# Keeping TensorE's instructions in emitted order in a fused block attention and feed-forward kernel

## The chip, the cores and the metric

The kernel runs on one core of one Trainium2 chip. The metric is device time in microseconds (us) of one execution; the time before is 1272.79 us, the median of 3 runs (1271.26 to 1273.68).

## The reference

Attention over 8 batches and 8 heads, 576 tokens, head size 64, with a mask by blocks of 64; its output, 4608 rows of 512, goes through a feed-forward layer with 2048 hidden units and a piecewise activation.

```python
def _attn_ref(q, k, v):                       # (8, 8, 576, 64), block = 64
    ...
    scores = scale * np.matmul(q, k.transpose(0, 1, 3, 2))
    ...
    mask = block_i >= block_j
    scores = np.where(mask, scores, -1000000000.0)
    scores = scores - np.max(scores, axis=-1, keepdims=True)
    attn = np.exp(scores)
    attn = attn / (np.sum(attn, axis=-1, keepdims=True) + 1e-09)
    return np.matmul(attn, v).astype(np.float32)

def _moe_ref(x, w_in, w_out):                 # (4608, 512), (512, 2048), (2048, 512)
    h = x @ w_in
    ...
    g = np.where(pos, h, np.where(neg, 0.0, (h + beta) ** 2 / (4.0 * beta)))
    return (g @ w_out).astype(np.float32)
```

The weights come as float64 and are converted on the core.

## The kernel before

The kernel works on 32 pairs of heads: 8 batches times 4 pairs. `attention_steps` is a generator that emits a pair in eight steps, each ended by a `yield`; work of the next pair (`nxt`) and the end of the last one (`old`) is mixed in by hand. The steps call these methods of `Pair`:

- `turned(is_q, j)`, line 341: four TensorE transposes (L346) of Q or K of head j into a PSUM tile `ps_qk`; ScalarE casts it to `qb` or `kb` (L351), and a DMA copies half of that to `qa` or `ka` (L357). `turned_last`, L365, does the last 64 rows of both heads.
- `scores(j, g)`, line 403: matmuls (L391, L394) into `ps_s`, VectorE's negated maximum (L414), ScalarE's exponential with its sum (L418), VectorE's reciprocal (L400, L401) and scaling (L424). From batch 1 on the result goes through a DMA to a rounded copy (`prr`, L246; in batch 1 `prs`, `pre` or the idle `vsr`, L239). `scores_last` is the same for the last 64 rows.
- `turn(j, g)` and `turn_last`: TensorE transposes of the probabilities (L461, in batch 0 L463) into `ps_t`, then a split into high and low parts on ScalarE (L454) and VectorE (L456).
- `attn_v` and `attn_v_first`: the weighted sums (L500) into `ps_av`, which become columns of `xh` and `xl`, the input of the feed-forward layer.

The feed-forward layer is a second generator. It works on chunks of 512 rows (9) and blocks of 128 hidden units (16 for each chunk). `ffn_in` is twelve matmuls (L646) into `ph`, then ScalarE (L655), VectorE (L656, L659), ScalarE (L660) and GpSimd (L661) make `gh` and `gl`, and a DMA fetches `wo` (L663). `ffn_out` is twelve matmuls (L670, L675) into four `po` banks. From the fifth step of the fifth pair on (`START`), one `ffn_in` or one `ffn_out` is emitted behind each attention step; what is left follows at the end. A third generator, `prepare_weights`, converts the weights (lines 152 to 184) beside batches 0 and 1 on ScalarE, VectorE and GpSimd.

PSUM has eight banks: three of the tag `work`, which `ps_qk`, `ps_s`, `ps_t` and `ps_av` take in turn, one for `ph`, four for `po` (lent to the attention before feed-forward begins). A tile gets its bank when the last reader of the bank's earlier tile is done.

The code only emits instructions. Their order on each engine's queue is set afterwards by an ordering tool: it takes, per engine, what it reckons to be ready first, by its own estimate of times, and otherwise what was emitted first. Each queue then runs strictly in that order. So an instruction can stand ahead of one that was emitted before it.

The sixth step of a pair is the one that the prediction speaks of most:

```python
            cur.scores(1, 1)
            cur.turn_last()
            if nxt:
                nxt.turned(False, 0)
            yield
```

Behind it the feed-forward generator emits twelve `ph` matmuls or twelve `po` matmuls.

Of the kernel before, what the change touches and what calls it, by code (L numbers as in the profile page):

```python
# [23 lines left out]
def block_attn_then_ffn(  # L24
# [59 lines left out]


    ident_f = ffn.tile([P, 512], F32, tag="t", name="ident_f")[:, :P]
    make_identity(nc, ident_f)
    ident_r = const.tile([P, P], F32R, tag="ident", name="ident_r")
    nc.vector.tensor_copy(ident_r, ident_f)
    ident = ident_r.bitcast(F32)  # L90

    xh = const.tile([P, NCC, RING], F32R, tag="xh", name="xh")
    xl = const.tile([P, NCC, RING], F32R, tag="xl", name="xl")
    wih = const.tile([P, NCC, DF], F32R, tag="wih", name="wih")
    wil = const.tile([P, NCC, DF], F32R, tag="wil", name="wil")
    wo_split = dram.tile([NFC, P, 2, DM], F32, tag="wo_split", name="wo_split")
# [3 lines left out]
    qa = const.tile([P, 2, QW], F32R, tag="qa", name="qa")  # L100
    qb = const.tile([P, 2, QW], F32R, tag="qb", name="qb")
    ka = const.tile([P, 2, S], F32R, tag="ka", name="ka")
    kb = const.tile([P, 2, S], F32R, tag="kb", name="kb")

    def last_blocks(t_):

        view = t_[:, :, SM : SM + BLK]
        if t_.shape[2] == S:
            return view
        part, (_, two), cols = view.ap  # L110
        return bass.AP(tensor=view.tensor, offset=view.offset, ap=[part, [QW + BLK, two], cols])


    mrow = att1.tile([NTL, 2, S], F32R, tag="pb0", name="mrow")


    pcs = [const.tile([P, 2, BLK], F32R, tag=f"pcs{i}", name=f"pcs{i}") for i in range(2)]
    vsr = [const.tile([P, NTL + 1, 2, D], F32R, tag=f"vsr{j}", name=f"vsr{j}") for j in range(2)]

    mtmp = ffn.tile([P, 512], F32, tag="t", name="mtmp")  # L120
    msel = ffn.tile([P, 512], F32, tag="t", name="msel")
    nc.vector.memset(mtmp, 0.0)
    nc.vector.memset(msel[:NTL], 0.0)
    nc.gpsimd.affine_select(
        out=msel[:NTL, : NTL * BLK].rearrange("p (t c) -> p t c", c=BLK),
        in_=msel[:NTL, : NTL * BLK].rearrange("p (t c) -> p t c", c=BLK),
        compare_op=ALU.not_equal, fill=1.0, base=0,
        pattern=[[-1, NTL], [0, BLK]], channel_multiplier=1,
    )
    sel = msel[:NTL, : NTL * BLK].rearrange("p (t c) -> p t c", c=BLK)  # L130
    for side in range(2):
        nc.vector.tensor_copy(mrow[:, side, :512], mtmp[:NTL, :512])
        nc.vector.tensor_copy(mrow[:, side, 512:S], mtmp[:NTL, : S - 512])
    rows = mrow[:, :, :SM].rearrange("p s (t c) -> p s t c", c=P)
    nc.vector.tensor_copy(rows[:, 0, :, :BLK], sel)
    nc.vector.tensor_scalar_mul(rows[:, 1, :, BLK:], sel, MASKED)
    for t_ in (qa, qb):
        nc.vector.tensor_copy(
            t_[:, :, SM:], mtmp[:, : 2 * (QW - SM)].rearrange("p (h c) -> p h c", h=2)
        )  # L140
    for t_ in pcs:
        nc.vector.tensor_copy(t_[BLK:], mtmp[BLK:, : 2 * BLK].rearrange("p (h c) -> p h c", h=2))
    for t_ in vsr:
        nc.vector.tensor_copy(
            t_[BLK:, NTL, :, :], mtmp[BLK:, : 2 * D].rearrange("p (h c) -> p h c", h=2)
        )
    for j in range(2):
        nc.sync.dma_start(qa[D:KA, j, :S].bitcast(F32), mrow[:, 0, :].bitcast(F32))
        nc.sync.dma_start(ka[D:KA, j, :].bitcast(F32), mrow[:, 1, :].bitcast(F32))


    def convert(n, source, hi, lo, done):

        if n < BORROW and n % 2:
            bits = ffn.tile([P, CW, 2], I32, tag="t", name="bits")
            work = ffn.tile([P, 2, CW], F32, tag="gl", name="work")
        else:
            bits = conv.tile([P, CW, 2], I32, tag="bits", name="bits")
            work = conv2.tile([P, 2, CW], F32, tag="work", name="work")
        nc.sync.dma_start(bits, source.bitcast(I32).rearrange("p (n t) -> p n t", t=2))  # L160
        top, mag = work[:, 0, :], work[:, 1, :].bitcast(U32)
        low = bits[:, :, 0]


        nc.scalar.mul(top, bits[:, :, 1].bitcast(F32), 2.0**-112)
        nc.scalar.mul(low, low.bitcast(U32), 2.0**-29)
        nc.vector.tensor_scalar(
            out=top, in0=top, scalar1=F32_TOP, scalar2=-F32_TOP, op0=ALU.min, op1=ALU.max
        )
        nc.vector.tensor_scalar(  # L170
            out=mag, in0=top.bitcast(U32), scalar1=3, scalar2=None, op0=ALU.logical_shift_left
        )
        nc.vector.scalar_tensor_tensor(
            out=mag, in0=top.bitcast(U32), scalar=0x80000000, in1=mag,
            op0=ALU.bitwise_and, op1=ALU.bitwise_or,
        )
        yield
        w32 = mag.bitcast(I32)
        nc.gpsimd.tensor_tensor(out=w32, in0=w32, in1=low, op=ALU.add)  # L179
        w32 = w32.bitcast(F32)  # L180
        nc.scalar.copy(hi(), w32)
        yield
        nc.gpsimd.tensor_tensor(out=lo(), in0=w32, in1=hi().bitcast(F32), op=ALU.subtract)
        if done:
            done()

    def weight_pieces():

        for f0 in range(0, DF, CW):
            fs = slice(f0, f0 + CW)  # L190
            for cc in range(NCC):
                yield (
                    w_in[cc * P : (cc + 1) * P, fs],
                    lambda cc=cc, fs=fs: wih[:, cc, fs], lambda cc=cc, fs=fs: wil[:, cc, fs], None,
                )
            for fc in range(f0 // P, (f0 + CW) // P):
                ws = {}

                def part(w, d0, ws=ws):
                    if not ws:  # L200
                        ws[0] = ffn.tile([P, 2, DM], F32R, tag="wo", name="ws")
                    return ws[0][:, w, d0 : d0 + CW]

                for d0 in range(0, DM, CW):
                    yield (
                        w_out[fc * P : (fc + 1) * P, d0 : d0 + CW],
                        lambda p_=part, d0=d0: p_(0, d0), lambda p_=part, d0=d0: p_(1, d0),
                        None if d0 + CW < DM else
                        lambda fc=fc, ws=ws: nc.sync.dma_start(wo_split[fc], ws[0].bitcast(F32)),
                    )  # L210

    def prepare_weights():

        live = []
        for n, piece in enumerate(weight_pieces()):
            live = [c for c in live + [convert(n, *piece)] if next(c, True) is None]
            yield
        for _ in range(LAG):
            live = [c for c in live if next(c, True) is None]
            yield  # L220
# [3 lines left out]
    spare = {"n": 0, "of": []}  # L224

    def as_float32r(src, plain):

        if plain:
            if not spare["of"]:
                spare["of"] = [t_[:, :NTL, :, :].rearrange("p t h d -> p (t h d)") for t_ in vsr]  # L230
                spare["of"].append(att1.tile([P, S], F32R, tag="x32", name="prs")[:, :TCH])
                spare["end"] = att1.tile([P, G0 + P], F32R, tag="pa11", name="pre")[:, :BLK]
            moved = [spare["of"][spare["n"] % 3]]
            spare["n"] += 1
            if src.shape[1] > TCH:
                moved.append(spare["end"])
            for i, dst in enumerate(moved):
                n = min(TCH, src.shape[1] - i * TCH)
                nc.sync.dma_start(dst[:, :n].bitcast(F32), src[:, i * TCH : i * TCH + n])  # L239
            return moved  # L240
        moved = []
        for c0 in range(0, src.shape[1], TCH):
            n = min(TCH, src.shape[1] - c0)
            pool, tag = ((conv, "bits"), (conv2, "work"))[c0 > 0]
            dst = pool.tile([P, TCH], F32R, tag=tag, name="prr")
            nc.sync.dma_start(dst[:, :n].bitcast(F32), src[:, c0 : c0 + n])  # L246
            moved.append(dst)
        return moved


    class Pair:


        GROUPS = (((0, 0), (1, P)), ((2, 0),), ((3, 0),))

        def __init__(self, b, hp):
            self.b, self.hp = b, hp

            self.plain = b < PLAIN
            self.first = b == 0 and hp == 0  # L260

# [467 lines left out]
    for _ in ffn_steps:  # L729
        pass  # L730
# [30 lines left out]
```

## Time and profile before

| | |
|---|---|
| median of 3 runs | 1272.79 us (1271.26 to 1273.68) |
| profiled execution | 1272.09 us, its span 1270.3 us |
| TensorE matmuls | 1210.7 us busy, 95% of the span |
| TensorE weight loads | 1018.4 us, 80% |
| VectorE / ScalarE / GpSimd | 856.4 / 701.3 / 456.3 us |
| granted TensorE clock, mean | 0.985 |

The page has one profiled execution. PE is TensorE's matmuls, PEld its weight loads, DVE VectorE, ACT ScalarE, POOL GpSimd, SP the queue that issues the DMAs. A row of the timeline has start, duration, engine, line, operation, output and inputs, the shape, how many such instructions are merged, and in brackets how long the engine stood idle before and who released it. Matmuls are pipelined: one that is shown as 0.39 us is followed by the next after 0.23, so "busy" overlaps and says that TensorE had work, not how fast it went.

### The profile page before, as it was taken

Reading aid. Unit: us, or ns where it says so; the run is one execution under the profiler, and the core shown is the slowest. Engines: PE = TensorE matmul, PEld = TensorE weight load, DVE = VectorE, ACT = ScalarE, POOL = GpSimd, SP = SyncE. Lnnn points to the kernel's source line nnn. Section 1 sums busy time; section 2 is a strip of 40 time slices with the busy share of each in tenths; the row PEclk is TensorE's granted clock in tenths of the full one; section 3 lists DMA queues with packets and bytes.
Section 4 is the critical chain, followed back from the end, with each engine's and each line's share of the span. In section 5 each row is a group of like instructions: output and inputs, shape, how many; then the busy total and the mean of one; then the engine's idle time right before and its main releaser. Section 6 shows DMA issues by size and latency. Waiting matters only on the chain.

```text
span 1270.3 us, 20591 instructions
## 1 busy us (share of the span) xinstructions
PE 1210.7 (95%) x6496; PEld 1018.4 (80%) x6496; DVE 856.4 (67%) x2164; ACT 701.3 (55%) x1827; POOL 456.3 (36%) x454
## 2 busy tenths in 40 slices
PE   5879887899999999999999999999999999999998
PEld 4667666688888888888888888888888888888886
DVE  8998877857776777777777777777777676222222
ACT  5877656546565655566556656555565564222222
POOL 3555655523332333333333333333333332222222
PEclk9888989899999999999999999999999999999999
DMA  5656666655444545564455545454445443322432
GB/s 157 182 165 213 196 228 210 212 184 173 148 152 147 191 144 161 158 193 149 148 162 168 178 141 161 153 181 143 152 154 184 151 132 117 127 92 97 133 100 100
DMA packets 146093, 201.30 MB, mean 158 GB/s; under 512 B 63152, under 2 KB 93872, under 8 KB 145984
## 3 DMA queue, kind: packets, MB, share of 16 engines
q1 hardware_dynamic: 145984, 199.98, 50.4%
q8 instruction: 52, 0.85, 0.3%
q14 instruction: 57, 0.47, 0.1%
HBM read 120.59 MB, written 17.83 MB: 109 GB/s over the span
## 4 chain that ended last, share of the span: by engine, by line
PE 68%; DVE 8%; ACT 4%; issue 3%; DMA 3%; POOL 2%; SPq 0%; ACTq 0%; POOLq 0%; DVEq 0%
PE ph L646 26%; PE po L670 16%; PE po L675 8%; PE ps_av L500 7%; PE ps_t L461 3%; PE ps_s L394 3%; PE ps_s L391 3%; ACT pr L418 2%; PE ps_qk L346 2%; DMA prr<-pr 2%; DVE t L656 2%; DVE nm L414 1%; DVE t L659 1%; DVE pr L424 1%; POOL work L179 1%
## 5 line engine op out<-in xcount | busy, mean ns | idle before, releaser
L661 POOL TENSOR_TENSOR gl<-t,gh 128x512 fp32r<-128x512 f32 x144 | 186.9, 1298 | 604.7 <-ACT gh L660 301.8
L670 PE MATMUL po<-wo,gh 128*128 128x512 f32 x1152 | 296.9, 399 | 0.1
L656 DVE SCALAR_TENSOR_TENSOR t<-t 128x512 f32<-128x512 f32 x144 | 112.9, 784 | 200.2 <-ACT t L655 198.5
L646 PE MATMUL ph<-xh,wih 128*128 128x512 f32 x576 | 237.6, 413 | 2.7 <-DVE t L659 1.8
L670 PEld LDWEIGHTS po<-wo,gh 128*128 128x128 f32 x1152 | 207.7, 188 | 39.3 <-ACT gh L660 0.6
L646 PE MATMUL ph<-xl,wih 128*128 128x512 f32 x576 | 227.4, 395 | 0.9 <-DVE xl L536 0.9
L646 PE MATMUL ph<-xh,wil 128*128 128x512 f32 x576 | 227.4, 395 | 0.0
L655 ACT ACTIVATE t<-ph 128x512 f32<-128x512 f32 x144 | 86.1, 598 | 184.7 <-PE ph L646 184.7
L418 ACT ACTIVATE pr<-ps_s,nm 128x128 f32<-128x128 f32 (+3 forms) x256 | 134.4, 529 | 50.6 <-DVE nm L414 50.3
L414 DVE TENSOR_REDUCE nm<-ps_s 128x1 f32<-128x128 f32 (+3 forms) x256 | 123.6, 485 | 48.7 <-PE ps_s L394 47.4
L675 PE MATMUL po<-wo,gl 128*128 128x512 f32 x576 | 155.3, 391 | 0.0
L660 ACT CAST gh<-t 128x512 fp32r<-128x512 f32 x144 | 89.6, 622 | 102.1 <-DVE t L659 101.7
L391 PE MATMUL ps_s<-ka,qa 68*128 68x288 f32 (+4 forms) x384 | 122.5, 334 | 9.1 <-ACT kb L351 4.2
L646 PEld LDWEIGHTS ph<-xh,wil 128*128 128x128 f32 x576 | 109.1, 189 | 24.1
L675 PEld LDWEIGHTS po<-wo,gl 128*128 128x128 f32 x576 | 108.1, 188 | 23.3
L646 PEld LDWEIGHTS ph<-xh,wih 128*128 128x128 f32 x576 | 109.1, 189 | 21.7 <-DVE t L659 2.4
L646 PEld LDWEIGHTS ph<-xl,wih 128*128 128x128 f32 x576 | 109.6, 190 | 20.2 <-DVE xl L536 1.5
L394 PE MATMUL ps_s<-kb,qb 128*128 128x288 f32 (+4 forms) x384 | 121.4, 323 | 0.0
L454 ACT CAST pb<-ps_t 128x512 fp32r<-128x512 f32 (+1 forms) x120 | 65.5, 546 | 85.6 <-PE ps_t L461 83.8
L424 DVE TENSOR_SCALAR pr<-pr,sm 128x128 f32<-128x128 f32 (+3 forms) x256 | 104.8, 430 | 4.0
L336 POOL TENSOR_TENSOR vsr<-vn,vsr 64x64 fp32r<-64x64 f32 (+1 forms) x96 | 72.8, 768 | 88.6 <-ACT vsr L335 88.6
L456 DVE TENSOR_TENSOR pb<-ps_t,pb 128x512 fp32r<-128x512 f32 (+1 forms) x120 | 75.6, 630 | 40.4 <-ACT pb L454 39.9
(101 smaller groups left out, 1961.4 us busy)
## 6 DMA issues: line engine op xcount, KB each, us to landing
wo<-wo_split SPq DMA_DIRECT2D x144, 512.0 KB, 3.4
prr<-pr SPq DMA_DIRECT2D x96, 192.0 KB, 2.7
prr<-pr SPq DMA_DIRECT2D x72, 256.0 KB, 2.6
out_dram<-ob SPq DMA_DIRECT2D x36, 256.0 KB, 3.9
qn<-in_q_dram SPq DMA_DIRECT2D x32, 256.0 KB, 2.9
kn<-in_k_dram SPq DMA_DIRECT2D x32, 256.0 KB, 2.9
bits<-in_moe_w_in_dram SPq DMA_DIRECT2D x32, 256.0 KB, 3.6
bits<-in_moe_w_out_dram SPq DMA_DIRECT2D x32, 256.0 KB, 3.2
```

The lines of the kernel that those rows point to most:

```text
L391: nc.tensor.matmul(ps, qa[:KA, j, c0 : c0 + P], ka[:KA, j, k0 : k0 + n], start=first, stop=False)
L394: nc.tensor.matmul(ps, qb[:, j, c0 : c0 + P], kb[:, j, k0 : k0 + n], start=False, stop=last)
L414: nc.vector.tensor_reduce(out=nm[:, i : i + 1], in_=ps[:, cs], axis=AX.X, op=ALU.max, negate=True)
L418: nc.scalar.activation(pr[:, cs], ps[:, cs], AF.Exp, bias=nm[:, i : i + 1], scale=1.0, accum_out=sm[:, i : i + 1],)
L424: nc.vector.tensor_scalar_mul(pr[:, cs], pr[:, cs], sm[:, i : i + 1])
L500: nc.tensor.matmul(ps[:, lo_col:], vt, x, start=first and i == 0 and m == 0, stop=last and i == len(parts) - 1 and m == len(mov) - 1,)
L646: nc.tensor.matmul(ph, w[:, cc, fs], x[:, cc, xs], start=(cc == 0 and i == 0), stop=(cc == NCC - 1 and i == 2),)
L656: nc.vector.scalar_tensor_tensor(out=t_, in0=t_, scalar=1.0, in1=t_, op0=ALU.min, op1=ALU.mult)
L660: nc.scalar.copy(gh, t_)
L661: nc.gpsimd.tensor_tensor(out=gl, in0=t_, in1=gh.bitcast(F32), op=ALU.subtract)
L670: nc.tensor.matmul(po[tt], gh[:, ts_], wo[:, w, :], start=(fc == 0 and w == 0), stop=False)
L675: nc.tensor.matmul(po[tt], gl[:, ts_], wo[:, 0, :], start=False, stop=fc == NFC - 1)
```

## The change

The body of the kernel, from the first tile to the last loop, is put into a context that tells the ordering tool to keep the emitted order on TensorE, for the whole program. Nothing is added or removed, and the code inside is only indented; each line number grows by one. The other queues are still ordered by the tool, which now reckons with TensorE's fixed order.

```diff
+    with tc.manual_schedule(engines={mybir.EngineType.PE}):
 ...
-    ident_f = ffn.tile([P, 512], F32, tag="t", name="ident_f")[:, :P]
+        ident_f = ffn.tile([P, 512], F32, tag="t", name="ident_f")[:, :P]
 ...
```

What moves on TensorE's queue: 6386 matmuls stand on it in both. In batches 2 to 7 one group of four moves in each pair, and the other four queues have the same rows in the same order there. In batches 0 and 1 more moves, and the other queues change too.

TensorE, the sixth step of a pair in batches 2 to 7, before. `ps_s` of 384 columns are the scores of `scores(1, 1)`, `ps_t` the transposes of `turn_last`, `ps_qk<-ks` those of `turned(False, 0)`, `ph` the matmuls of `ffn_in`, of which twelve belong to this step:

```order
L391 MATMUL ps_s<-ka,qa 128x384
L394 MATMUL ps_s<-kb,qb 128x384
L461 MATMUL ps_t<-ident_r,prr 128x128 x4
L461 MATMUL ps_t<-ident_r,prr 64x128
L646 MATMUL ph<-xh,wih 128x512
L646 MATMUL ph<-xl,wih 128x512
L646 MATMUL ph<-xh,wil 128x512
L646 MATMUL ph<-xh,wih 128x512
L646 MATMUL ph<-xl,wih 128x512
L646 MATMUL ph<-xh,wil 128x512
L346 MATMUL ps_qk<-ident_r,ks 128x128 x4
```

The same place now:

```order
L392 MATMUL ps_s<-ka,qa 128x384
L395 MATMUL ps_s<-kb,qb 128x384
L462 MATMUL ps_t<-ident_r,prr 128x128 x4
L462 MATMUL ps_t<-ident_r,prr 64x128
L347 MATMUL ps_qk<-ident_r,ks 128x128 x4
L647 MATMUL ph<-xh,wih 128x512
L647 MATMUL ph<-xl,wih 128x512
L647 MATMUL ph<-xh,wil 128x512
```

The K transposes moved ahead of six `ph` matmuls; in 17 of the 23 pairs it is six, in the other 6 it is seven. Behind them all twelve `ph` follow.

TensorE in batch 0, second pair, before. Here `turn(0, 2)` has its `ps_t` at L463, and three `ph` of the first `ffn_in`, which is emitted in the fifth pair, stand among the attention of the second:

```order
L346 MATMUL ps_qk<-ident_r,qs 128x128 x4
L646 MATMUL ph<-xh,wih 128x512
L646 MATMUL ph<-xl,wih 128x512
L463 MATMUL ps_t<-ident_r,pr 128x128 x4
L391 MATMUL ps_s<-ka,qa 128x384
L394 MATMUL ps_s<-kb,qb 128x384
L646 MATMUL ph<-xh,wil 128x512
```

The same place now:

```order
L464 MATMUL ps_t<-ident_r,pr 128x128 x4
L347 MATMUL ps_qk<-ident_r,qs 128x128 x4
L392 MATMUL ps_s<-ka,qa 128x384
L395 MATMUL ps_s<-kb,qb 128x384
L464 MATMUL ps_t<-ident_r,pr 128x128 x4
```

The transposes of Q moved behind those of `turn(0, 2)`. The twelve `ph` of the first `ffn_in`, three in each of the second to the fifth pair, moved together to the fifth step of the fifth pair, where they are emitted.

TensorE in batch 1, fourth pair, second step, before (`po` are the twelve matmuls of `ffn_out`, `ps_av` the weighted sums):

```order
L461 MATMUL ps_t<-ident_r,prs 128x128 x4
L391 MATMUL ps_s<-ka,qa 128x384
L394 MATMUL ps_s<-kb,qb 128x384
L365 MATMUL ps_qk<-ident_r,qs 128x128
L365 MATMUL ps_qk<-ident_r,ks 128x128
L646 MATMUL ph<-xh,wih 128x512
```

The same place now:

```order
L462 MATMUL ps_t<-ident_r,prs 128x128 x4
L671 MATMUL po<-wo,gh 128x512 x8
L676 MATMUL po<-wo,gl 128x512 x4
L392 MATMUL ps_s<-ka,qa 128x384
L395 MATMUL ps_s<-kb,qb 128x384
L366 MATMUL ps_qk<-ident_r,qs 128x128
L366 MATMUL ps_qk<-ident_r,ks 128x128
```

The twelve `po` moved ahead of the scores; before, they stood behind seven `ph` and six weighted sums.

More of the change, by code (lines that the diff above doesn't have):

```diff
@@ L141, in block_attn_then_ffn @@
[L141 to L194, printed above, removed]
-                )
[L196 to L209, printed above, removed]
-                    )
@@ L212, in prepare_weights @@
[L212 to L248, printed above, removed]
@@ L496, in weighted @@
-        def weighted(self, ps, j, parts, first=True, last=True):
-            for i, (kt, lo_col, mov) in enumerate(parts):
-                vt = self.vs[j][: (BLK if self.plain and kt == NTL else P), kt, :, :]
-                for m, x in enumerate(mov):
-                    nc.tensor.matmul(
-                        ps[:, lo_col:], vt, x,
-                        start=first and i == 0 and m == 0,
-                        stop=last and i == len(parts) - 1 and m == len(mov) - 1,
-                    )
@@ new lines, in block_attn_then_ffn @@
+        START = 8 * NPAIR + 4
+        GROUP = CW // P
+        PART = NCC + GROUP * DM // CW
+        EARLY = 24
+        LAG = 2
+        weights = prepare_weights()
+        ffn_steps = feed_forward()
+        converted = 0
+        for i, _ in enumerate(attention_steps()):
+            if i < START:
+                want = (i + 1) * EARLY // START
+            else:
+                want = max(
+                    EARLY + (i - START + 1) * (NFC // GROUP * PART - EARLY) // (2 * NFC - 4 * GROUP),
+                    ((i - START) // (2 * GROUP) + 1) * PART,
+                )
+            want += LAG
+            for _ in range(want - converted):
+                next(weights, None)
+            converted = max(converted, want)
+            if i >= START:
+                banks["free"] = False
+                next(ffn_steps, None)
```

981 lines of the change are left out of this document (529 added, 452 removed).

## The prediction

> **What bounds the kernel now.** I read the page first: busy shares, the slices over time, and the chain that ended last.
>
> ```profile
> PE 1210.7 (95%) x6496; PEld 1018.4 (80%) x6496; DVE 856.4 (67%) x2164; ACT 701.3 (55%) x1827; POOL 456.3 (36%) x454
> PE   5879887899999999999999999999999999999998
> PEclk9888989899999999999999999999999999999999
> PE 68%; DVE 8%; ACT 4%; issue 3%; DMA 3%; POOL 2%; SPq 0%; ACTq 0%; POOLq 0%; DVEq 0%
> ```
>
> TensorE is 95% busy and holds 68% of the chain, but not evenly: the first nine slices (about 290 us) have gaps and a lower clock, the rest has neither. So I cut the span into five stretches: the attention before feed-forward begins, the rest of the fifth pair, where it begins, then up to the first moved K transposes of batch 2, from there to the end of attention, and feed-forward alone.
>
> ```profile
> 0.00:112.00 112.00, 84.36 (x440) 68.39 (x440) 99.45 (x307) 81.63 (x245) 55.92 (x76) 0.91 0.60 174
> 112.00:126.00 14.00, 12.83 (x64) 10.30 (x65) 11.40 (x33) 10.96 (x32) 5.92 (x7) 0.88 0.66 222
> 126.00:290.00 164.00, 145.87 (x716) 115.47 (x716) 123.60 (x303) 96.92 (x271) 84.96 (x99) 0.96 0.64 203
> 290.00:1064.00 774.00, 766.40 (x4376) 658.09 (x4375) 561.90 (x1428) 460.11 (x1190) 261.97 (x237) 1.00 0.51 159
> 1064.00:1271.00 207.00, 201.19 (x904) 166.16 (x903) 60.03 (x97) 51.65 (x92) 47.54 (x37) 1.00 0.33 108
> ```
>
> The columns after the length are PE, PEld, DVE, ACT and POOL busy, the granted clock, DMA. In the first, VectorE is busy 99.45 of 112 us and TensorE 84.36: there TensorE waits for others. From 290 to 1064 us TensorE is busy 766.40 of 774 us at the full clock, VectorE 562: any microsecond that TensorE loses there is added to the end. Its waits in that stretch, from the view of waits (longest in total first, weight loads):
>
> ```profile
> PEld ps_qk L346 <- ACT pr L418: 10.7, 20, 0.7
> PEld ps_t L461 <- PE ps_s L394: 2.7, 4, 1.0
> PEld ps_t L461 <- ACT pr L418: 2.0, 2, 1.5
> ```
>
> One wait stands out, 20 times about half a microsecond: the transposes of K (L346) for ScalarE's exponential (L418). That is exactly the place which the change moves. Here is one instance, from the timeline:
>
> ```profile
> 626.14 0.34 PE L394 MATMUL ps_s<-kb,qb 128*128 128x384 f32 x1
> 626.32 0.52 PE L461 MATMUL ps_t<-ident_r,prr 128*128 128x128 f32 x5
> 626.67 0.46 PE L646 MATMUL ph<-xh,wih 128*128 128x512 f32 x1
> 626.98 0.40 PE L646 MATMUL ph<-xl,wih 128*128 128x512 f32 x1
> 627.11 0.55 DVE L414 TENSOR_REDUCE nm<-ps_s 128x1 f32<-128x384 f32 x1
> 627.70 0.58 ACT L418 ACTIVATE pr<-ps_s,nm 128x384 f32<-128x384 f32 x1 [0.29 <-DVE nm L414]
> 627.90 0.40 PE L646 MATMUL ph<-xh,wil 128*128 128x512 f32 x1
> 628.18 0.19 ACT L418 ACTIVATION_READ_ACCUMULATOR pr<-ps_s,nm 128x1 f32 x1
> 628.42 0.40 PEld L346 LDWEIGHTS ps_qk<-ident_r,ks 128*128 128x128 f32 x4 [0.56 <-ACT pr L418]
> 628.80 0.47 PE L646 MATMUL ph<-xh,wih 128*128 128x512 f32 x1
> 630.03 0.40 PE L646 MATMUL ph<-xh,wil 128*128 128x512 f32 x1
> ```
>
> The three `work` banks of PSUM rotate. The scores at 626.14 took one, the two `ps_t` tiles at 626.32 the others, so the K transposes need the bank of the scores, and it is free only when the exponential has read it, at 628.37. In between TensorE ran six `ph` matmuls (626.67 to 627.90, one per 0.23 us), then waited the remaining half microsecond.
>
> **The change in batches 2 to 7.** The emitted order has no `ph` between the `ps_t` transposes and the K transposes. The release at 628.37 does not depend on the `ph`: reduction and exponential hang on the scores of 626.14 alone, and on rows of VectorE and ScalarE that stand in the same order as before. So TensorE reaches the K transposes at about 626.65 and stands until 628.42, 1.8 us in place of 0.56; then all twelve `ph` follow in place of six. The end of the twelfth moves by six spacings, 6 x 0.23 = 1.37 us. Queued behind the wait are the twelve `ph`, the next scores and the weighted sums; ScalarE's L655 and the rest of the feed-forward chain wait for the `ph` and shift as a whole. The transposes issue no DMA; the copy of K that follows their cast starts as long after the scores as before.
>
> Some pairs hoisted seven `ph`:
>
> ```profile
> 559.34 0.53 PE L461 MATMUL ps_t<-ident_r,prr 128*128 128x128 f32 x5
> 559.70 0.45 PE L646 MATMUL ph<-xh,wih 128*128 128x512 f32 x1
> 560.96 0.20 ACT L418 ACTIVATION_READ_ACCUMULATOR pr<-ps_s,nm 128x1 f32 x1
> 561.15 0.39 PE L646 MATMUL ph<-xh,wih 128*128 128x512 f32 x1
> 561.20 0.50 PEld L346 LDWEIGHTS ps_qk<-ident_r,ks 128*128 128x128 f32 x4
> 561.38 0.46 PE L346 MATMUL ps_qk<-ident_r,ks 128*128 128x128 f32 x4
> ```
>
> Here the bank was free at 561.16, just before TensorE came, so the K transposes can start 0.18 us earlier than they did, and seven spacings (1.61) come behind them: +1.43 us; where the release came later than this it is the full 1.6. How many pairs there are: the transposes of L346 for K in this stretch are
>
> ```profile
> L346 PE MATMUL ps_qk<-ident_r,ks x184: 221/248/285, 290.9 to 1044.1; 128*128 128x128 f32 x184
> ```
>
> 184 = 23 pairs x 2 heads x 4, and one of the two heads is moved in each (the other already stands where it was emitted). By the order seventeen of the 23 had six `ph` ahead, six had seven: 17 x 1.37 + 6 x 1.5 = 32.3 us; in two of the seventeen the bank was free a tenth of a microsecond early, which takes off 0.2. I take **+32**. It is given back only if another TensorE wait shrinks: the other waits of the stretch are small (2.7, 2.0 and less above) and start from TensorE's own scores, so I count nothing. The far ends: if the release came as early as the bare reduction and exponential allow after the scores (0.34 + 0.55 + 0.58 + 0.19 = 1.66 us after 626.14, so 0.57 us sooner than now), the 23 waits would be 0.57 shorter, 13 us in all: +19. Above, +32 plus the clock (below).
>
> On gaps the row of 626 to 628 is to be weighed against the Trainium skill, "TensorE: Matmul & The Clock Gate", section "Why this matters for your kernels": keep gaps between bursts of matmuls under about 3 us, or the clock halves. By that rule gaps of 1.8 us are free of any further price and +32 stands.
>
> **The change in the first 290 us.** Two terms. First, the first feed-forward unit:
>
> ```profile
> 0.00:112.00 112.00, 4.34 (x12) 1.95 (x12) 0.91 0.60 174
> ```
>
> Its twelve `ph` (this view is of L646 alone) ran in gaps of the first 112 us; now they stand in the pair at 112 to 126 us, where TensorE is busy 12.83 of 14 us. They cost from 0 (into its waits) over 2.7 us (12 x 0.23) to 5.2 (at half clock, 0.43 each, below). I take 2. What leaves the first 112 us gains nothing, since TensorE waits there; nor do the scores that now stand ahead of the K transposes. Second, from 126 to 290 us, 29 matmuls of `ph` and `po` that were hoisted over late transposes and weighted sums go back behind them: at most 29 x 0.23 = 6.7 us. Against that, twelve `po` now stand ahead of these scores, which waited long:
>
> ```profile
> 222.51 0.29 PEld L391 LDWEIGHTS ps_s<-ka,qa 68*128 68x128 f32 x1 [4.03 <-ACT kb L351]
> ```
>
> They may fill up to 12 x 0.23 = 2.8 us of it, or wait for their own `wo`. From -2.8 to +6.7 I take +2, for TensorE idles 18 of 164 us there and later waits take up part of a delay. VectorE's, ScalarE's, GpSimd's and SP's rows change their order here too (conversions against softmax); no row prices that, I give it +-6. Together **+4**, between -8 and +17.
>
> **Sum.** The profiled execution took 1272.1 us (span 1270.3): 1272.1 + 32 + 4 = 1308.1. The median shown is 0.7 above it: **1309 us**.
>
> **Rivals.**
> *Half clock.* The granted clock dropped after stretches in which TensorE streamed little:
>
> ```profile
> 177.73:181.14 3.41, 1.36 (x6) 0.84 (x6) 3.38 (x6) 1.87 (x6) 3.41 (x5) 1.00 0.91 290
> 181.14:184.55 3.41, 3.14 (x6) 2.16 (x7) 3.41 (x9) 1.35 (x6) 2.70 (x3) 0.50 0.17 55
> 205.04:208.45 3.41, 2.41 (x13) 1.76 (x14) 3.34 (x10) 1.75 (x6) 2.62 (x4) 1.00 0.86 270
> 181.41 0.90 PE L500 MATMUL ps_av<-pb,vs 128*128 128x320 f32 x1 [1.80 <-ACT pr L418]
> ```
>
> Six matmuls in 3.41 us (four `ph`, two transposes), with a wait of 1.80, were followed by 3.41 us at 0.50; thirteen in 3.41 us were not. In the changed kernel TensorE streams nothing but nine transposes from 626.31 to 628.80; a stretch of 3.41 us around this has room for (3.41 - 2.49) / 0.23 = 4 large matmuls: at the edge. If it trips, it does so for the 27% of the pairs whose 3.41 us contain the whole gap (0.92 / 3.41), six pairs, each losing half of 3.41 us: +10, **1319 us**. For it: the row of 181.14, which the rule quoted above would not give (its wait is 1.80 us). Against: the nine transposes may count as work. The same page, section "PE-mode transpose", says that transposes do not count as busy in the same way, which speaks for this rival.
>
> *Faster.* The first 290 us contain 47 us in which TensorE is idle (290 - 84.36 - 12.83 - 145.87); the emitted order puts ready scores ahead of transposes that wait, as at 222.51. Were all 47 us given back, the time would be 1272.8 + 32 - 47 = **1258 us**; it decides from 35 us on, three quarters of it. Against it: VectorE is busy 99.45 of the first 112 us, which no order of TensorE shortens.
>
> *A dear opening.* If the waits at the late transposes add up and the other queues turn worse, the opening costs 13 in place of 4: **1318 us**.
>
> *Shorter release.* +19 in place of +32, the far end above: **1296 us**.
>
> *No change.* TensorE's new waits would have to be hidden; with 766.40 of 774 us busy nothing hides them. **1273 us.**
>
> **How the numbers follow.** Forecast, 1302 to 1315: 0.58. Half clock 0.20, a dear opening 0.09, shorter release 0.06, faster 0.04, no change 0.03. Within 0.2% is what a measurement of this kernel cannot tell from no change. So faster 0.04, same 0.03, slower 0.93. The range leaves out the two last and the lower half of the release case, and half of a dear opening that also trips the clock: 1298 to 1324.
>
> **What would show it.** In the changed profile: the wait of the K transposes for L418 at about 1.7 us, 23 times, some 40 us in all in place of 10.7; twelve `ph` in one run behind them; TensorE's busy time from 290 us to the last pair unchanged, that stretch 32 us longer; the granted clock 1.00 in it (else the first rival). The tail of feed-forward alone stays at 207 us. I am wrong if the exponential releases the bank at another distance from the scores, or if the first 290 us change by more than 10 us.

## The result, and the profile after

The changed kernel takes 1331.66 us (1328.48 to 1334.08) against 1272.59 us for the kernel before, run on the same chip: a ratio of 1.0463, with an interval of 1.0433 to 1.0493. It is 59 us slower; 36 were forecast. Lines of the changed code are one higher than before (L346 is L347, L418 is L419). Its profiled execution took 1329.46 us, the span 1327.7. Both profiles have 6496 matmul records on TensorE, not the 6386 given with the change. Of all runs named below one, of e10_turned_fill, took 2360.20 us, nearly twice the three others of that kernel, and no figure here contains it. The page of the changed kernel, busy time and the two rows of TensorE over the slices:

```profile
PE 1223.2 (92%) x6496; PEld 1033.5 (78%) x6496; DVE 850.7 (64%) x2164; ACT 702.0 (53%) x1827; POOL 456.0 (34%) x454
PE   5866988899999999999999999999999999999998
PEclk9888988999999999999999999999999999999999
```

To see where the 57.4 us between the two spans lie, I cut both at the same two points: the first and the last of the moved K transposes. The view by stretches of the kernel before, with the columns as in the prediction:

```profile
0.00:290.90 290.90, 243.97 (x1222) 194.86 (x1223) 235.34 (x643) 190.41 (x550) 146.80 (x181) 0.94 0.63 193
290.90:1043.90 753.00, 746.99 (x4271) 641.56 (x4270) 545.47 (x1390) 447.60 (x1156) 256.39 (x231) 1.00 0.52 160
1043.90:1270.30 226.40, 219.69 (x1007) 182.01 (x1005) 75.56 (x133) 63.26 (x123) 53.12 (x42) 1.00 0.33 108
```

And of the changed kernel:

```profile
0.00:304.00 304.00, 242.54 (x1215) 196.46 (x1215) 231.73 (x642) 191.64 (x550) 146.75 (x181) 0.92 0.60 184
304.00:1101.00 797.00, 760.76 (x4275) 654.72 (x4276) 543.49 (x1390) 446.87 (x1156) 256.19 (x231) 0.98 0.49 152
1101.00:1327.70 226.70, 219.90 (x1008) 182.34 (x1007) 75.48 (x133) 63.46 (x123) 53.05 (x42) 1.00 0.33 108
```

The opening is 13.1 us longer, the steady part 44.0, the end 0.3. The row of the steady part splits further by itself. TensorE's idle time there went from 753.00 - 746.99 = 6.0 to 797.00 - 760.76 = 36.2 us: 30.2 us of waiting. Its busy time went up by 13.8 us for the same matmuls, and the granted clock from 1.00 to 0.98: the work itself ran slower. One pair of the changed kernel shows both, in the timeline of TensorE:

```profile
691.45 0.34 PE L395 MATMUL ps_s<-kb,qb 128*128 128x384 f32 x1
691.63 0.53 PE L462 MATMUL ps_t<-ident_r,prr 128*128 128x128 f32 x5
693.81 0.54 PE L347 MATMUL ps_qk<-ident_r,ks 128*128 128x128 f32 x4 [1.65 <-ACT pr L419]
694.72 0.40 PE L647 MATMUL ph<-xh,wil 128*128 128x512 f32 x1
694.95 0.40 PE L647 MATMUL ph<-xh,wih 128*128 128x512 f32 x1
696.42 0.63 PE L647 MATMUL ph<-xl,wih 128*128 128x512 f32 x1
696.85 0.63 PE L647 MATMUL ph<-xh,wil 128*128 128x512 f32 x1
```

The K transposes wait 1.65 us for the exponential. All 23 of them, in the view of waits from 250 to 1130 us:

```profile
PEld ps_qk L347 <- ACT pr L419: 39.2, 23, 2.1
```

That is the wait that was forecast. But from 695.2 us on the same `ph` matmul comes every 0.43 us in place of 0.23. The stretches around it, of 3.41 us each:

```profile
691.81:695.22 3.41, 1.76 (x14) 1.43 (x13) 2.70 (x9) 1.99 (x5) 0.00 (x0) 1.00 0.66 211
695.22:698.64 3.42, 3.42 (x10) 2.68 (x9) 0.00 (x0) 0.00 (x0) 0.00 (x0) 0.50 0.35 101
698.64:702.05 3.41, 3.41 (x23) 3.07 (x22) 2.72 (x7) 2.56 (x6) 0.00 (x0) 1.00 0.00 0
```

TensorE was busy 1.76 of 3.41 us, and the next 3.41 us were granted half the clock. After 304 us there are eight such stretches, at 340.2, 517.7, 695.2, 801.0, 838.6, 910.3, 1016.1 and 1087.8 us; half of 3.41 us each makes 13.7 us, the 13.8 of the busy time. Before, there was none in this part.

### The profile page after: what moved, and what is told of

It is laid out like the page before. It is cut to its first block, busy times and chain, and to the rows that moved or that the text cites. A ratio compares the mean times of both kernels' runs of the same rounds, so it can differ in the third digit from the quotient of the medians.

```text
span 1327.7 us, 20572 instructions
## 1 busy us (share of the span) xinstructions
PE 1223.2 (92%) x6496; PEld 1033.5 (78%) x6496; DVE 850.7 (64%) x2164; ACT 702.0 (53%) x1827; POOL 456.0 (34%) x454
## 4 chain that ended last, share of the span: by engine, by line
PE 67%; DVE 10%; ACT 5%; DMA 3%; issue 3%; POOL 1%; SPq 0%; ACTq 0%; POOLq 0%; DVEq 0%
PE ph L647 28%; PE po L671 15%; PE po L676 7%; PE ps_av L501 7%; PE ps_t L462 3%; ACT pr L419 3%; PE ps_s L395 2%; PE ps_s L392 2%; PE ps_qk L347 2%; DMA prr<-pr 2%; DVE t L657 2%; DVE nm L415 1%; DVE pr L425 1%; DVE t L660 1%; DVE sm L401 1%
## 5 line engine op out<-in xcount | busy, mean ns | idle before, releaser
L647 PE MATMUL ph<-xh,wih 128*128 128x512 f32 x576 | 242.9, 422 | 0.7 <-DVE sm L401 0.7
L647 PE MATMUL ph<-xh,wil 128*128 128x512 f32 x576 | 233.1, 405 | 0.0
L647 PE MATMUL ph<-xl,wih 128*128 128x512 f32 x576 | 232.3, 403 | 0.0
L419 ACT ACTIVATE pr<-ps_s,nm 128x128 f32<-128x128 f32 (+3 forms) x256 | 134.1, 526 | 55.5 <-DVE nm L415 53.6
L647 PEld LDWEIGHTS ph<-xh,wil 128*128 128x128 f32 x576 | 112.8, 196 | 26.2
L647 PEld LDWEIGHTS ph<-xl,wih 128*128 128x128 f32 x576 | 113.6, 197 | 21.0
L647 PEld LDWEIGHTS ph<-xh,wih 128*128 128x128 f32 x576 | 112.9, 196 | 21.4 <-DVE sm L401 0.8
```

Source lines behind the costliest of these rows:

```text
L419: nc.scalar.activation(pr[:, cs], ps[:, cs], AF.Exp, bias=nm[:, i : i + 1], scale=1.0, accum_out=sm[:, i : i + 1],)
L647: nc.tensor.matmul(ph, w[:, cc, fs], x[:, cc, xs], start=(cc == 0 and i == 0), stop=(cc == NCC - 1 and i == 2),)
```

## The experiments

All times stand against runs of the kernel before on the same chip; the column on the right is the ratio less one, times 1272 us.

| kernel | median us | ratio, interval | us |
|---|---|---|---|
| e1_six_ahead | 1288.58 | 1.0135, 1.0118 to 1.0152 | +17 |
| e2_from_batch2 | 1315.49 | 1.0348, 1.0325 to 1.0372 | +44 |
| e3_filled | 1317.36 | 1.0371, 1.0354 to 1.0389 | +47 |
| e17_half_filled | 1316.91 | 1.0352, 1.0332 to 1.0373 | +45 |
| e10_turned_fill | 1317.92 | 1.0359, 1.0335 to 1.0384 | +46 |
| e4_twelve_ahead | 1278.76 | 1.0067, 1.0042 to 1.0092 | +9 |
| e6_batch0 | 1276.03 | 1.0047, 1.0028 to 1.0066 | +6 |
| e7_fifth_pair | 1280.64 | 1.0083, 1.0064 to 1.0102 | +11 |
| e8_rest_batch1 | 1276.17 | 1.0043, 1.0028 to 1.0058 | +5 |
| e9_unit_ahead | 1331.92 | 1.0462, 1.0427 to 1.0498 | +59 |
| e12_fill_opening | 1333.55 | 1.0483, 1.0459 to 1.0507 | +61 |
| e14_qk_early | 1334.44 | 1.0499, 1.0478 to 1.0521 | +63 |
| e16_twelve_b1 | 1279.31 | 1.0058, 1.0040 to 1.0076 | +7 |
| e13_unit_and_twelve | 1268.59 | 0.9991, 0.9978 to 1.0005 | -1 |
| e15_all_three | 1279.96 | 1.0076, 1.0059 to 1.0092 | +10 |
| e18_unit_in_gaps | 1282.11 | 1.0083, 1.0066 to 1.0100 | +11 |
| e5_tool_twelve | 1263.58 | 0.9940, 0.9920 to 0.9960 | -8 |
| e11_tool_twelve_b1 | 1259.41 | 0.9906, 0.9892 to 0.9921 | -12 |

### Are there two losses?

One kernel undoes the steady part, the other the opening. In e1 the K transposes are handed to `ffn_in`, which emits them behind its sixth matmul:

```diff
                 cur.turn_last()
-                if nxt:
+                if nxt and cur.b >= 2:
+                    held.append(nxt)
+                elif nxt:
                     nxt.turned(False, 0)
...
+                    if held and 3 * cc + i == 5:
+                        held.pop().turned(False, 0)
```

> The changed kernel, but in batches 2 to 7 six matmuls of ph are emitted ahead of the K transposes that the change had moved, so that this spot is as it was before; the opening stays as changed. Theory of two separate losses (the K transposes' wait with the half clock that it trips from 290 us on, 44 us, and the opening, 13 us): the moved pairs lose nothing, the exponential's wait is back to about 10.7 us in all, no record at half clock between 300 us and the last pair, and 12 to 13 us stay from the opening: 1284 to 1286 us. Rival, a loss that does not hang on this spot (a lower clock or slower issue in the whole program that goes with the fixed order): 1315 to 1330 us. Rival, the loss of the opening is what makes the later waits long: also above 1300.

In e2 the context stands around the steps of the main loop from step 64 (batch 2) on only:

```diff
+        with tc.manual_schedule(engines={mybir.EngineType.PE}) if 64 <= i < 1000000 else nullcontext():
```

> The kernel before, with the emitted order on TensorE kept only from batch 2 on; in the first two batches all queues are as before. Theory of two losses: the opening ends as before (first moved K transposes at about 291 us), then 29 us of waits and 12 to 14 us of half clock in the moved pairs and 3 at the end: 1314 to 1318 us. Rival, the opening's loss comes from the same waits and goes with them: 1328 to 1334. Rival, the half clock of the steady part was started by the opening: 1300 to 1304, with no half-clock record after 300 us.

The steady part in the two, by stretches, cut as above, e1 first:

```profile
310.10:1064.50 754.40, 747.60 (x4272) 641.67 (x4272) 544.92 (x1390) 447.52 (x1156) 256.28 (x231) 1.00 0.52 160
```

```profile
0.00:291.50 291.50, 243.36 (x1216) 193.40 (x1216) 235.80 (x642) 190.53 (x550) 147.41 (x181) 0.94 0.62 192
291.50:1090.00 798.50, 761.66 (x4277) 654.69 (x4278) 543.72 (x1390) 447.82 (x1156) 256.34 (x231) 0.98 0.48 151
```

With six `ph` ahead, the steady part is back to 754.4 us at the full clock. With the tool's opening and the fixed order behind it, it has the whole 798.5. The two losses, 17 and 44 us, add up to the change's 59 within the intervals: they are separate. The theory's size for the opening was too small, 12 to 13 us against 17.

### Wait and clock taken apart

e3, e17 and e10 leave the useful matmuls where the change put them, and fill the wait with work whose result is overwritten: six matmuls, three, or sixteen transposes.

```diff
+            if held:
+                for _ in range(6):
+                    nc.tensor.matmul(ph, wih[:, 0, fs], xh[:, 0, xs], start=True, stop=True)
+                held.pop().turned(False, 0)
...
```

> The changed kernel, and in batches 2 to 7 six more matmuls of 128x512, whose result is overwritten, ahead of the K transposes: 23 x 6 matmuls of work added, the useful ones left where the change put them. Theory (a wait of 1.8 us that streams nothing costs its own length, and in the stretches with too little streaming half of 3.4 us more): the added work lies in the wait and costs nothing, the eight half-clock records after 300 us go, 13 us less than the changed kernel: 1316 to 1320 us. Rival, the half clock comes of the nine transposes in a row, not of the gap: 1329 to 1334. Rival, the added matmuls are paid in full, 23 x 1.37 us on top: 1350 to 1365.

> The changed kernel, and in batches 2 to 7 three more matmuls of 128x512 ahead of the K transposes, so that about 1.1 us of the wait of 1.8 are left. Theory that what trips the clock is the share of idle time in a stretch of 3.4 us, and that 1.1 us is below it: no half-clock record after 300 us, 1316 to 1320 us as with six. Rival, any wait of over a microsecond trips it: six to nine records, 1328 to 1334. The wait itself costs the same in both, since the useful ph stand behind it.

In e10 the line in the loop is `nc.tensor.transpose(ph[:, :P].bitcast(F32R), ident_r, ident_r)`, 16 times.

> The changed kernel, with sixteen transposes of 128x128 ahead of the moved K transposes in batches 2 to 7, into the ph tile that is overwritten behind them: the wait is filled as with the six matmuls, but with transposes. Theory that transposes don't count as streaming for the clock: the half-clock records after 300 us stay, seven to nine, and so does the time, 1328 to 1334 us. Rival, any instruction on TensorE counts: none is left, 1316 to 1320 us. If the sixteen don't fit into the wait, up to 10 us more by both.

The steady part of e3, then of e17:

```profile
304.70:1089.50 784.80, 778.46 (x4409) 667.53 (x4409) 544.61 (x1390) 447.53 (x1156) 256.32 (x231) 1.00 0.50 154
```

```profile
307.00:1091.60 784.60, 764.55 (x4343) 655.10 (x4343) 544.23 (x1390) 447.43 (x1156) 256.53 (x231) 1.00 0.50 154
```

Both are 784.7 us long, 31.7 more than before and 12.3 less than the changed kernel, at the clock 1.00. So the waits cost 32 us and the clock 12, and the 138 added matmuls of e3 cost nothing. What e17 still waits, in its view of waits from 300 to 1130 us:

```profile
PE ps_qk L347 <- ACT pr L419: 18.3, 23, 1.3
```

0.8 us per pair and 1.3 at most, less than the 1.1 that I had reckoned with, and no half-clock record after 300 us. Only one of the 23 waits is over a microsecond, so the rival of e17, that any such wait trips the clock, is not tested by it. e10 went against my theory. One of its pairs, in the timeline of TensorE:

```profile
340.27 0.53 PE L462 MATMUL ps_t<-ident_r,prr 128*128 128x128 f32 x5
340.64 1.52 PE L651 MATMUL ph<-ident_r 128*128 128x128 f32 x16
342.74 0.54 PE L347 MATMUL ps_qk<-ident_r,ks 128*128 128x128 f32 x4 [0.58 <-ACT pr L419]
```

And the stretch of 3.41 us with this pair in it, and the next:

```profile
339.71:343.12 3.41, 2.83 (x30) 2.61 (x28) 3.06 (x9) 1.51 (x6) 0.99 (x1) 1.00 0.51 174
343.12:346.53 3.41, 3.41 (x17) 2.84 (x17) 0.52 (x3) 0.93 (x2) 0.00 (x0) 1.00 0.39 124
```

Most of the 2.83 us are transposes, and the next stretch has the full clock; there is no half-clock record after 300 us. In this wait transposes keep the clock up as matmuls do. What trips it here is the idle time, not the kind of instruction around it.

### All twelve ahead

As e1, with `== 11` in place of `== 5`: the K transposes stand behind the whole run of `ph`.

> The changed kernel, but in batches 2 to 7 all twelve matmuls of ph are emitted ahead of those K transposes. Theory of waits: the bank is free 0.5 to 0.8 us before TensorE comes, the wait of 10.7 us that the kernel before still had is gone as well, and nothing behind is late: 1274 to 1278 us, the 12 us of the opening being left. Rival, K's cast and copy come 1.4 us later and the scores of the next pair wait for them: 1284 to 1290 us. By both, no half clock between 300 us and the last pair.

```profile
308.10:1050.40 742.30, 740.92 (x4266) 641.69 (x4265) 549.33 (x1385) 445.09 (x1154) 259.36 (x231) 1.00 0.52 162
```

TensorE is busy 740.92 of 742.30 us; the wait that the kernel before still had is gone as well, and nothing behind it is late. What is left of its loss is the opening.

### The opening, by place

Three kernels keep the emitted order in one part of the opening only, as e2 does from step 64 on.

> The kernel before, with the emitted order on TensorE only in the first four pairs (batch 0, the first 112 us). Theory that the opening's loss is mostly the fifth pair's: 1273 to 1277 us (up to 5 us that the changed kernel was late at the fourth pair, partly given back). Rival, order in batch 0 puts the other queues in a worse order for good and so makes the fifth pair late: 1280 to 1288.

> The kernel before, with the emitted order on TensorE only in the fifth pair, where feed-forward begins (its first unit's twelve ph, that ran in gaps of batch 0, stand in this pair too). Theory that this pair is where the opening is lost (in the changed kernel it took 12 us longer, with waits of 4 and 5 us for work of ScalarE and VectorE and three to four stretches at half clock): 1280 to 1286 us. Rival, the loss was handed down from batch 0: 1271 to 1275. The pair's twelve ph alone would be 2.7 us at the full clock, 5.4 at half.

> The kernel before, with the emitted order on TensorE only in the sixth to eighth pair (the rest of batch 1). Theory that the opening's loss is the first five pairs': 1268 to 1275 us, about 4 us of the K transposes' own waits against 4 that these pairs gave back in the changed kernel. Rival, each stretch of the opening costs alike: 1276 to 1280.

The fifth pair is the dearest, +11, as the theory had it; but the other two cost +6 and +5, and e8 came out as its rival had it. The fifth pair in TensorE's timeline, first of the kernel before, then of e7:

```profile
113.07 0.80 PE L646 MATMUL ph<-xh,wih 128*128 128x512 f32 x1 [1.75 <-DVE t L659]
117.66 0.45 PE L461 MATMUL ps_t<-ident_r,prs 128*128 128x128 f32 x4
120.33 0.51 PE L346 MATMUL ps_qk<-ident_r,ks 128*128 128x128 f32 x4
```

```profile
118.44 0.72 PE L461 MATMUL ps_t<-ident_r,prs 128*128 128x128 f32 x4 [5.91 <-DMA prs<-pr]
119.47 0.76 PE L646 MATMUL ph<-xh,wih 128*128 128x512 f32 x1
```

Before, twelve `ph` of the second unit ran while the copy for the transposes of `prs` was on its way (113.07 to 117.6). In the emitted order the transposes stand in front: TensorE waits 5.91 us, and the first unit's `ph` begin only then.

### The opening, by cause

In e9 the first unit is emitted ahead of `turn(0, 2)` in the fifth pair; in e12 matmuls that nobody reads stand ahead of the waiting transposes; in e14 the next pair's Q and K transposes for its second head stand ahead of `attn_v_first` in batches 0 and 1.

```diff
                 cur.scores(1, 0)
+                if i == NPAIR:
+                    next(ffn_steps)
                 cur.turn(0, 2)
...
```

> The changed kernel, with the first feed-forward unit's twelve ph emitted one turn earlier in the fifth pair: ahead of the four transposes of prs, which wait for a copy by DMA, instead of behind them. Theory that the fifth pair loses because TensorE stands at these transposes with ready ph behind them (3.9 us here, 5.9 where only this pair keeps the emitted order): the wait is filled and the kernel is 4 to 7 us faster than the changed one: 1323 to 1328 us. Rival, the pair is held by ScalarE's and VectorE's queues and the wait moves to the K transposes behind (5.2 us there now): 1330 to 1334.

> The changed kernel, with eight matmuls of 128x256, whose result nobody reads, ahead of each of three groups of late transposes in the second to fifth pair, where TensorE waits 1.4 to 5.5 us: about 0.9 us of added work each at the full clock. Theory that about half of the opening's loss is half clock (15 such stretches of 3.4 us before 290 us against 11 in the kernel before, each up to 1.7 us): three to six stretches fewer, 2 to 7 us less than the changed kernel: 1324 to 1330 us. Rival, the opening is bound by the other engines, and the clock is a bystander: 1330 to 1334. Rival, the added matmuls are in the way: 1335 to 1345.

> The changed kernel; in the first two batches the next pair's transposes of Q and K for its second head are emitted ahead of the pair's first weighted sums, and so ahead of the next pair's scores, as the tool had them in the first pairs. Theory that the next pair's operands came late because their transposes stood behind weighted sums that wait: the kernel is 4 to 8 us faster than the changed one, 1323 to 1328 us. Rival, the places of these transposes don't matter, and the loss is in the waits for softmax: 1330 to 1334. Rival, the tool's place was right only together with its other hoists: 1334 to 1340.

All three missed: none gave anything back. So neither the wait that e9 fills nor the place of the transposes in e14 is by itself the cause. e12 says little about the clock, for its matmuls did not raise it: up to 300 us it has 14 stretches of 3.41 us at half clock, the changed kernel 15, the kernel before 11. e14 has 23 of them and is only 4 us slower than the changed kernel, so eight more of them cost some 4 us at most there, unless that move gave something back at the same time; what the four more of the changed kernel cost was not measured. In e9 the fifth pair itself was shorter (105.2 to 140.0 us against 104.8 to 145.6 in the changed kernel), but the sixth was as much longer. Two more kernels took the waits away in combination: e16 has all twelve `ph` ahead of K's transposes from batch 1 on (`cur.b >= 1`), e13 that and e9's move, e15 these and e14's.

> The fixed order with twelve ph ahead of K's transposes in batches 1 to 7, the first unit's ph left where the change put them. To be held against the same with batches 2 to 7 alone (1279 us) and against both moves (1269 us). Theory that the wait at K's transposes is the one that nothing behind it can absorb: 1268 to 1272 us. Rival, the two moves are needed together, since each wait filled alone comes back at the other: 1275 to 1280.

> The fixed order with all that filled its long waits from the fifth pair on: the first unit's ph ahead of the waiting transposes of prs, and twelve ph ahead of K's transposes in batches 1 to 7. To be held against the kernel with the fixed order and twelve ahead from batch 2 on (1279 us). Theory that the opening's loss is the sum of TensorE's long waits (5.2 and 2.4 us at K's transposes, 3.9 at those of prs): 1268 to 1272 us. Rival, these waits are symptoms, and the chain through the other queues sets the pace: 1275 to 1280.

> The fixed order with the first unit's ph ahead, twelve ph ahead of K's transposes from batch 1 on, and the next pair's Q and K transposes ahead of the weighted sums in the first two batches. Theory that the opening's loss has these two parts: 1262 to 1268 us, close to the tool's order with twelve ahead (1259). Rival, nothing is left to gain from these moves: as the kernel without the early Q and K transposes, 1270 to 1280.

e16 gained next to nothing over e4 (+7 against +9), e13 gained 8 us over e16. The timeline of TensorE in the fifth pair says why, here of the changed kernel:

```profile
121.05 0.72 PE L462 MATMUL ps_t<-ident_r,prs 128*128 128x128 f32 x4 [3.86 <-ACT bits L167]
132.46 0.72 PE L347 MATMUL ps_qk<-ident_r,ks 128*128 128x128 f32 x4 [5.25 <-ACT pb L455]
```

Of e16:

```profile
121.00 0.72 PE L462 MATMUL ps_t<-ident_r,prs 128*128 128x128 f32 x4 [3.91 <-ACT bits L167]
132.63 0.80 PE L651 MATMUL ph<-xh,wih 128*128 128x512 f32 x1 [5.42 <-DVE t L666]
```

And of e13:

```profile
124.40 0.50 PE L653 MATMUL ph<-xh,wih 128*128 128x512 f32 x1 [0.17 <-DVE t L668]
137.66 0.53 PE L347 MATMUL ps_qk<-ident_r,ks 128*128 128x128 f32 x4 [1.04 <-ACT qb L352]
```

With K's transposes out of the way, the second unit's `ph` wait at the same place, until the same time: they need the one `ph` bank, which VectorE's maximum frees behind the first unit. Only when the first unit starts early as well is the bank free at 124.4, and the wait goes. So two waits stood side by side, and taking K's transposes away alone uncovered the other. The other way round it is less plain: in e9 the wait at K's transposes in the fifth pair is 1.57 us in place of 5.25, and what was gained is lost in the sixth pair, where weighted sums wait 3.08 us and K's transposes 2.68 us. e15 shows that the early Q and K transposes do harm here, +11 over e13.

The last kernel tried to put the first unit's `ph` back into batch 0, three per pair ahead of `turn(0, 0)`.

> The fixed order with twelve ph ahead of K's transposes from batch 1 on (1279 us), and the first unit's twelve ph emitted three per pair in the second to fifth pair, ahead of the first late transposes of each, about where the tool had put them. Theory that the fifth pair's waits come of the first unit starting late, since the second unit's ph need its bank (one buffer, freed by VectorE's maximum): the wait of 5.4 us is gone and the time is at most that of the kernel which moves the whole unit ahead of the transposes of prs, 1262 to 1269 us. Rival, in that kernel it was the order within the fifth pair that mattered: 1273 to 1280.

It missed, and does not answer its question: at the place that I chose TensorE waited for the sums of the pair before, in the view of waits from 14 to 300 us

```profile
PE ph L581 <- ACT xh L536: 7.9, 4, 3.7
PE ph L581 <- DVE xl L537: 4.9, 4, 2.2
```

12.8 us in all, of which the kernel before had 0.9 at its first unit's `ph`.

### A version that beats both

e5 and e11 leave all queues to the tool, as before, and emit K's transposes behind the twelve `ph`, from batch 2 and from batch 1 on.

> The kernel before (the ordering tool on all queues), with K's transposes emitted behind the twelve matmuls of ph in batches 2 to 7. Theory of waits: the opening is that of before, and the moved spot loses the 10.7 us of waits that it had; the steady part was 9.3 us shorter than before with the emitted order and twelve ahead, and 3 us less at the end: 1258 to 1262 us, faster than both kernels. Rival, those 12 us were a property of the fixed order (fewer matmuls hoisted elsewhere): 1268 to 1273.

> As the kernel with the ordering tool and twelve ph ahead of K's transposes, but from batch 1 on instead of batch 2. Theory: in batch 1 the K transposes waited about a microsecond per pair in the kernel before; 2 to 4 us less than with batch 2 alone: 1259 to 1262 us. Rival, in batch 1 VectorE and ScalarE set the pace, and K's cast, now later, is waited for: 1263 to 1268.

```profile
0.00:288.70 288.70, 240.23 (x1228) 192.02 (x1229) 238.50 (x646) 191.45 (x551) 146.93 (x181) 0.95 0.64 196
288.70:1031.50 742.80, 740.36 (x4266) 641.49 (x4265) 548.85 (x1385) 444.62 (x1154) 259.61 (x231) 1.00 0.52 162
```

e11 takes 1259.41 us, 0.9906 of the kernel before: the steady part is 10 us shorter (742.8 against 753.0), and the opening, where the fixed order loses, is the tool's. e5 came a little above what I expected; its profiled opening ended at 293.9 us against 290.9, of which 1.4 are the six `ph` that now stand ahead of that mark.

## Why the prediction was wrong

*The waits (+32): right.* The wait was forecast at 1.7 us, 23 times, some 40 us in all, and the row says 39.2 and 23. Idle time rose by 30.2 us; with the clock taken out (e3, e17) the steady part is 31.7 us longer. The bank rotation, the distance from scores to release (2.23 us in the pair at 626.14 us before, 2.31 in the one at 691.45 now, where the exponential's last row ends at 693.76) and the six or seven spacings behind the wait held. The far end of a shorter release did not come.

*The clock: the rival was true, and its price too low.* It was given 0.20 and 10 us; it came, with 13.8. Two steps failed. I held against it that the nine transposes may count as work; e10 shows that they do count, and it tripped all the same, since the wait alone was enough. And I took it that a stretch trips only if it holds the wait and the nine transposes whole, 2.49 us, in 27% of the pairs: six. The wait alone is what it has to hold: in the changed kernel the stretches that tripped after 304 us had TensorE busy 1.84 us or less of 3.41, and those that hold the whole wait of 1.65 us have about 1.76. A stretch that falls at random holds it in (3.41 - 1.65) / 3.41 = 52% of the pairs, twelve; ten had 1.84 us or less, and eight of these tripped. Two stretches of the changed kernel show that this is at the edge, and that the edge is not one sharp number; the first was followed by one at half clock (1016.1 us), the second was not:

```profile
1012.66:1016.07 3.41, 1.84 (x15) 1.55 (x14) 3.38 (x12) 2.36 (x8) 0.63 (x1) 1.00 0.62 148
551.87:555.28 3.41, 1.74 (x10) 1.52 (x11) 2.43 (x8) 1.93 (x5) 0.00 (x0) 1.00 0.65 211
```

In the opening the busy time sorts the stretches less well still. The first of these, of the kernel before, was followed by half clock, the second, of the changed kernel, was not:

```profile
157.26:160.67 3.41, 2.08 (x14) 1.50 (x14) 3.27 (x9) 2.81 (x10) 2.64 (x3) 1.00 0.77 252
193.48:196.89 3.41, 1.54 (x6) 1.14 (x7) 3.29 (x8) 2.03 (x7) 1.38 (x2) 1.00 0.77 202
```

So the wait is what tripped the clock in batches 2 to 7, since filling it (e3, e10, e17) took all eight stretches away; by what measure the clock decides is not shown. I had quoted a stretch of the kernel before (177.73 us) that had 1.36 us busy and was followed by half clock, and let a rule weigh more than it. The Trainium skill, "TensorE: Matmul & The Clock Gate", section "Why this matters for your kernels", asks for gaps under about 3 us; here a gap of 1.65 us was enough, and the measurement decides. Its section "PE-mode transpose" says that transposes do not count as busy in the same way; in e10 they did (the trace calls them MATMUL and names no mode).

*The opening (+4): the term was mis-sized, 13 us in the profiled run, 15 to 16 between kernels that differ in it alone (the changed kernel and e2, e4 and e5).* The failing step is "They cost from 0 ... to 5.2 ... I take 2". It priced the twelve `ph` of the first unit as TensorE's time where they now stand. Their price is in what hangs on them: in a fixed order they stand behind transposes that wait for a copy, so the whole chain of the first unit (`ph`, Relu, maximum, the one `ph` bank) starts late, and the second unit waits for it (e16, 5.42 us). With the same twelve ahead from batch 1 on, the fixed order (e16) is 19 us slower than the tool's (e11); moving the first unit (e13) takes 8 of these away. Of the 11 that remain batch 0 makes about 6 (e6); what makes them there, and where the other 5 lie, is not shown: e14 and e18 only say what does not give them back, and the clock of the opening stays an open rival, since e12 left it as it was. The prediction's ±6 for the other queues, "no row prices that", was the honest part of this term, and too narrow; I named ten microseconds as the point at which I would be wrong, and it was passed.

*The sum.* Waits, clock and opening do not exclude each other, but the rivals were written as if they did: the half clock at 1319, a dear opening at 1318, and the case of both only by half, at the range's upper end. From the rows above: 1272.1 + 30.2 + 13.8 + 13.1 + 0.3 = 1329.5, the profiled execution's 1329.46. What was excluded was the sum of two cases that had each been seen.

*The end of the program* was to stay, and did (0.3 us). That nothing would be given back, and that no rival of the faster side would come, was right.

## What to carry to other kernels

A fixed order on the engine that bounds the kernel turns each instruction that waits into a stop for all that stands behind it; before fixing it, look at each wait for what ready work the tool had moved in front, and emit that work there. Price a moved group by the chain that starts with it and the buffer that the chain holds, not by its own busy time, and when two waits end at about the same time, take both away before judging either. Costs that can come together are added before a range is given, and here the best order was the tool's with one emission moved (0.9906), not the fixed one.

## What the hardware showed that I had not expected

The granted clock goes by stretches of 3.41 us: after 300 us the eight half-clock records of the changed kernel start whole multiples of 3.41 us apart (52 between the first two, 104 from the first to the third), whatever the work. A stretch in which TensorE is idle for 1.65 us, a little under half, can cost the next one half its speed, 1.7 us, as much as the wait itself; waits of 0.8 us and up to 1.3 (e17) never did in 23 pairs. In e9 eight half-clock stretches in a row began 71.68 us apart, from 484.1 to 985.9 us: that is 21 stretches and two pairs, so the pairs and the stretches had fallen into step. And sixteen transposes that fill this wait protect the clock as well as six large matmuls do.
